# Moving the FFN row products of a decode kernel into a loop pass that skips its V products, with a new load order and a buffer of its own for w_down

## Chip, cores and metric

One core of a Trainium2 chip. The batches of experiments ran on different chips, so the ratios are to the kernel before in the same rounds. The metric is the device time of one execution in microseconds, median of several runs. "Span" is the time from the first to the last instruction of an execution; it is about 1.8 us less than the execution's time.

## The reference

A decode step for one token: grouped-query attention over a cache of 32768 positions, a SwiGLU FFN, and a sigmoid gate that mixes the two.

```python
g = sigmoid((x * gate_w).sum(-1))                    # x: 512 numbers
q = x @ wq                                           # 32 heads of 128, 8 K/V heads
a = softmax(q k^T / sqrt(128)) v @ wo                # k, v: 8 x 32768 x 128 each, bf16
b = (silu(x @ w_gate) * (x @ w_up)) @ w_down         # F = 1792
out = g * a + (1 - g) * b
```

K and V are 134 of the 148 MB that the kernel must read. Each number is used by four heads and then never again.

## The kernel before

Everything is loaded through one queue, in the order of the list `stream`. K and V come in halves of 4 MB, written K(g,half) and V(g,half) for K/V head g. Five buffers of 4 MB (the ring) take them in turn; an entry of the stream may be issued only when the entry that had its buffer before has been used up (`before` and `released`).

```python
    stream = [("wq",), ("F1",), ("K", 0, 0), ("K", 0, 1), ("F2",)]
    for g in range(1, G):
        for hf in range(2):
            stream += [("K", g, hf), ("V", g - 1, hf)]
    stream += [("V", G - 1, 0), ("V", G - 1, 1), ("wo",)]

    place = {("wq",): 1, ("F1",): 3, ("F2",): 4, ("wo",): 2}
    for g in range(G):
        for hf in range(2):
            place["K", g, hf] = 2 * hf
            place["V", g, hf] = 2 * hf + 1
    place["V", G - 1, 1] = 0
    before = {}
    for i, e in enumerate(stream):
        for d in stream[:i]:
            if place[d] == place[e]:
                before[e] = d
```

```python
            def _(sp):
                for i, e in enumerate(stream):
                    ld = sem_ld[place[e]]
                    if e in before:
                        sp.wait_ge(*released[before[e]])
    # ... cut ...
                    else:
                        kind, g, hf = e
                        src = (A_k_cache if kind == "K" else A_v_cache)[
                            0, g, hf * (S // 2) : (hf + 1) * (S // 2), :
                        ].rearrange("(p r) d -> p r d", r=RH)
                        dst = kv_slot(e)
    # ... cut ...
```

PE (TensorE) first forms q, then the FFN rows (`emit_ffn`, 32 matmuls), then runs a loop over the heads. In each pass it transposes a K half, forms the scores, and then does the V products of the previous head. In the first pass there is no previous head, so the V products are skipped.

```python
                def emit_ffn():
                    take(load_sem(("F1",)), 32)
                    for acc, wt in ((ps_g, wg), (ps_u, wu)):
                        for k in range(KC):
                            for c in range(4):
                                ins = pe.matmul(
                                    acc[32 * c : 32 * c + 1, :],
                                    xT[:, k : k + 1],
                                    wt[:, k, c * FW : (c + 1) * FW].rearrange(
                                        "d (i j) -> d j i", j=FC
                                    ),
                                    start=(k == 0),
                                    stop=(k == KC - 1),
                                )
                    ins.then_inc(sem_pe_h, 1)
```

```python
                emit_x()
                pe.wait_ge(sem_xT, 1)
                pe.wait_ge(sem_ident, 2)
                pe.wait_ge(sem_osel, 1)
                emit_q()
                emit_ffn()
                pe.sem_inc(sem_pv, 2)
                pe.wait_ge(sem_tT, 1)
                with pe.Fori(0, G) as g:
                    emit_k(0)
                    with pe.If(g > 0):
                        emit_pv(0)
                    emit_k(1)
                    with pe.If(g > 0):
                        emit_pv(1)
                    pe.sem_inc(sem_exp, -2)
                    pe.wait_ge(sem_ptc, 2)
                    pe.sem_inc(sem_ptc, -2)
                    pe.sem_inc(sem_qc, -1)
```

ACT takes the sigmoid of the FFN rows and DVE the two products and a transpose, all ahead of their own loops:

```python
                act.wait_ge(sem_qz, 4)
                emit_qc(0)
                act.wait_ge(sem_pe_h, 1)
                act.activation(sg[:, :], ps_g, ACT.Sigmoid).then_inc(sem_sg, 1)
```

```python
                dve.wait_ge(sem_sg, 1)
                dve.tensor_tensor(t1[:, :], sg[:, :], ps_g, ALU.mult).then_inc(sem_t1, 1)
                dve.wait_ge(sem_t1, 1)
                dve.wait_ge(sem_omg, 1)
                dve.scalar_tensor_tensor(
                    tr[:, :], t1[:, :], omg[:, 0:1], ps_u, ALU.mult, ALU.mult
                ).then_inc(sem_t1, 1)
                dve.wait_ge(sem_t1, 2)
                dve.transpose(tT[:, :], tr[:, :]).then_inc(sem_tT, 1)
```

After the loop come the last head's V products, the w_down products (`emit_outb`), and 64 matmuls against wo.

## Time and profile before

| | |
|---|---|
| time, median of 3 runs | 355.69 us (355.57 to 355.91) |
| the execution that was traced | 358.45 us, span 356.6 us |
| share of the span: PE, DVE, load queue | 72%, 56%, 97.1% |

Two lines of the profile page of before: busy time of PE (microseconds, share of the span), and the load queue (packets, MB, share of what 16 DMA engines could have done in the span).

```profile
PE 257.4 (72%) x2467; PEld 182.1 (51%) x2467; DVE 200.4 (56%) x373; ACT 18.5 (5%) x54; POOL 5.6 (2%) x22
...
q1 hardware_dynamic: 6050, 148.12, 97.1%
```

The chain of waits that ended last, as shares of the span by line:

```profile
by line: DMA ring<-in_A_wo_dram 7.3%; PE ps L442 2.2%; PE ps L456 0.6%; SPq L331 0.5%; DVE ktT L733 0.3%; issue 0.2%; DVE row L817 0.1%; PE ps L576 0.1%; PE ps L488 0.1%
```

The queue is nearly always busy, and the last thing that the kernel waited for was a load. So the time is that of the load stream, plus whatever stops the stream. The windows of 1 us show where it stops. Columns: start and end, length, busy time of PE, PE's weight loads, DVE, ACT and POOL with instruction counts, PE clock, DMA share, GB/s.

```profile
43.00:44.00 1.00, 1.00 (x13) 0.42 (x12) 1.00 (x2) 0.00 (x0) 0.00 (x0) 1.00 1.02 430
44.00:45.00 1.00, 1.00 (x12) 0.99 (x10) 1.00 (x3) 0.00 (x0) 0.00 (x0) 1.00 0.45 186
...
46.00:47.00 1.00, 1.00 (x14) 0.70 (x7) 0.88 (x3) 0.00 (x0) 0.00 (x0) 1.00 0.00 0
...
50.00:51.00 1.00, 0.94 (x8) 0.61 (x6) 1.00 (x3) 0.00 (x0) 0.00 (x0) 1.00 0.37 131
```

The last column goes from 430 to 0, and stays at 0 from 46 to 49 us. The timeline says why (start, length, engine, line, operation, count, idle time before it):

```profile
22.89 6.64 PE L411 MATMUL ps<-ring,xT 128*1 128x448 bf16 x32 [0.43 <-PEq L360]
...
31.52 0.65 DVE L722 STREAM_TRANSPOSE tT<-tr 128x448 bf16<-128x448 bf16 x1
...
32.60 4.50 PE L442 MATMUL ps<-ident_f,ring 128*128 128x128 f32 x20 [3.07 <-PEq L360]
...
48.77 0.33 SPq L349 DMA_DIRECT2D ring<-in_A_k_cache_dram  x1
```

The FFN rows occupy PE from 22.89 us for 6.64 us, the transpose of their product on DVE ends at 32.2 us, and only then does K(0,0) start on PE (line 442). K(1,0), which needs the buffer of K(0,0), is issued at 48.77 us. All that could be issued ahead of it, 18.1 MB, had landed by about 46 us.

The end of the kernel: the second half of the last V (line 507) is multiplied when it lands at 343.84 us, then the last o product (line 522), the 64 wo matmuls (line 576), and the output's issue.

```profile
343.84 1.04 PE L507 MATMUL ps<-ring,ET 128*16 128x512 bf16 x16 [2.23 <-DMA ring<-in_A_v_cache_dram]
...
346.02 1.84 PE L522 MATMUL ps<-osel,pv_sb 128*128 128x4 f32 x8 [1.14 <-PEq L360]
...
349.31 5.30 PE L576 MATMUL ps<-ring,O 128*1 128x256 bf16 x64 [0.67 <-DMA ring<-in_A_wo_dram]
...
355.10 0.31 SPq L351 DMA_DIRECT2D out_dram<-row  x1
```

From that landing to the output's issue it is 355.10 - 343.84 = 11.3 us. I call it the tail.

One more line is used throughout, the stretch from 44 to 74 us, in which the hole and its refilling lie:

```profile
44.00:74.00 30.00, 26.85 (x239) 19.96 (x238) 25.97 (x48) 3.20 (x7) 0.39 (x1) 0.94 0.85 356
```

### The profile page before, as it was taken

Reading aid. Unit: us, or ns where it says so; the run is one execution under the profiler, and the core shown is the slowest. Engines: PE = TensorE matmul, PEld = TensorE weight load, DVE = VectorE, ACT = ScalarE, POOL = GpSimd, SP = SyncE. Lnnn points to the kernel's source line nnn. Section 1 sums busy time; section 2 is a strip of 40 time slices with the busy share of each in tenths; the row PEclk is TensorE's granted clock in tenths of the full one; section 3 lists DMA queues with packets and bytes.
Section 4 is the critical chain, followed back from the end, with each engine's and each line's share of the span. In section 5 each row is a group of like instructions: output and inputs, shape, how many; then the busy total and the mean of one; then the engine's idle time right before and its main releaser. Section 6 shows DMA issues by size and latency. Waiting matters only on the chain. (4 is left out here: it accounts for less than half of the span.)

```text
span 356.6 us, 5752 instructions
## 1 busy us (share of the span) xinstructions
PE 257.4 (72%) x2467; PEld 182.1 (51%) x2467; DVE 200.4 (56%) x373; ACT 18.5 (5%) x54; POOL 5.6 (2%) x22
## 2 busy tenths in 40 slices
PE   0086987968669783959296775869594948887756
PEld 0043755836466453736183746656372727654343
DVE  2224688856647582839275574838382845766211
ACT  1000000300100001000100001000100010001000
POOL 0200000000000000000000000000000000000000
PEclk9997699898958996999989896978899895999687
DMA  8999959999999999999999999999999999999994
GB/s 338 404 425 459 387 196 411 452 426 419 456 419 423 452 419 441 437 415 445 434 415 448 434 412 448 434 412 448 434 412 448 434 412 452 430 415 452 408 421 197
DMA packets 6060, 148.21 MB, mean 416 GB/s; under 512 B 675, under 2 KB 678, under 8 KB 1062
## 3 DMA queue, kind: packets, MB, share of 16 engines
q1 hardware_dynamic: 6050, 148.12, 97.1%
q8 instruction: 5, 0.08, 0.1%
q14 instruction: 1, 0.01, 0.0%
q10 hardware_dynamic: 4, 0.00, 0.0%
HBM read 148.11 MB, written 0.00 MB: 415 GB/s over the span
## 5 line engine op out<-in xcount | busy, mean ns | idle before, releaser
L733 DVE COPY ktT<-ps 128x1024 bf16<-128x1024 bf16 x256 | 162.8, 684 | 89.5 <-PE ps L442 86.4
L442 PE MATMUL ps<-ident_f,ring 128*128 128x128 f32 x1024 | 159.6, 312 | 54.9 <-PEq L360 54.9
L442 PEld LDWEIGHTS ps<-ident_f,ring 128*128 128x128 f32 x1024 | 134.4, 162 | 91.8 <-issue 66.3
L456 PE MATMUL ps<-ktT,qc 128*32 128x512 bf16 x512 | 42.5, 409 | 15.2 <-DVE ktT L733 15.1
L507 PE MATMUL ps<-ring,ET 128*16 128x512 bf16 x512 | 32.3, 394 | 4.0 <-DMA ring<-in_A_v_cache_dram 2.2
L507 PEld LDWEIGHTS ps<-ring,ET 128*16 128x16 bf16 x512 | 12.6, 91 | 20.0 <-issue 7.4
L456 PEld LDWEIGHTS ps<-ktT,qc 128*32 128x32 bf16 x512 | 8.0, 95 | 28.4 <-DVE ktT L733 24.1
L738 DVE TENSOR_REDUCE pmaxf<-ps 128x1 f32<-128x512 f32 x16 | 11.1, 692 | 13.8 <-DVEq L737 13.8
L522 PEld LDWEIGHTS ps<-osel,pv_sb 128*128 128x128 f32 x80 | 14.2, 266 | 2.2 <-issue 2.2
L522 PE MATMUL ps<-osel,pv_sb 128*128 128x4 f32 x80 | 13.7, 294 | 1.6 <-PEq L360 1.6
L596 ACT ACTIVATE qc<-qz 128x112 bf16<-128x112 bf16 x8 | 2.4, 296 | 212.3 <-DVE nbias L756 199.5
L618 ACT ACTIVATE P<-ps,nbias 128x512 bf16<-128x512 f32 x16 | 10.7, 675 | 27.4 <-DVE nbias L756 27.4
L769 DVE COPY pv_sb<-ps 128x512 f32<-128x512 f32 x10 | 6.8, 682 | 6.0 <-PE ps L507 6.0
L386 PE MATMUL ps<-xT,ring 128*128 128x1 bf16 x128 | 3.6, 165 | 7.4 <-PEq L360 7.4
L488 PE MATMUL ps<-ident,P 128*128 128x128 bf16 x72 | 7.0, 220 | 1.9 <-ACT P L618 1.4
L763 DVE COPY ET<-ps 128x512 bf16<-128x512 bf16 x18 | 7.5, 415 | 1.3 <-PE ps L488 1.3
L302 POOL PARTITION_ALL_REDUCE gmax<-pmax x8 | 3.0, 373 | 309.9 <-DVE pmax L745 309.9
L386 PEld LDWEIGHTS ps<-xT,ring 128*128 128x128 bf16 x128 | 3.5, 104 | 7.4 <-issue 7.4
L411 PE MATMUL ps<-ring,xT 128*1 128x448 bf16 x32 | 6.6, 984 | 0.4 <-PEq L360 0.4
L488 PEld LDWEIGHTS ps<-ident,P 128*128 128x128 bf16 x72 | 5.4, 98 | 2.8 <-ACT P L618 1.9
L369 PE MATMUL ps<-ones_bf,x_row 1*128 1x1 bf16 x4 | 0.3, 174 | 8.7 <-DMA gw_row<-in_gate_w_dram 8.7
L576 PE MATMUL ps<-ring,O 128*1 128x256 bf16 x64 | 5.2, 334 | 0.7 <-DMA ring<-in_A_wo_dram 0.7
(75 smaller groups left out, 39.0 us busy)
## 6 DMA issues: line engine op xcount, KB each, us to landing
ring<-in_A_k_cache_dram SPq DMA_DIRECT2D x16, 4096.0 KB, 25.2
ring<-in_A_v_cache_dram SPq DMA_DIRECT2D x15, 4096.0 KB, 32.9
ring<-in_A_wq_dram SPq DMA_DIRECT2D x1, 4096.0 KB, 13.4
ring<-in_A_v_cache_dram SPq DMA_DIRECT2D x2, 2048.0 KB, 27.2
ring<-in_A_wo_dram SPq DMA_DIRECT2D x1, 2048.0 KB, 22.8
ring<-in_B_w_gate_dram SPq DMA_DIRECT2D x1, 1792.0 KB, 17.3
ring<-in_B_w_up_dram SPq DMA_DIRECT2D x1, 1792.0 KB, 21.1
ring<-in_B_w_down_dram SPq DMA_DIRECT2D x1, 1792.0 KB, 43.4
```

Of the source, the lines that this page charges most:

```text
L386: ins = pe.matmul(ps_m[:, M_Q0 + h : M_Q0 + h + 1], wq_v[:, c, h * DH : (h + 1) * DH], xT[:, c : c + 1], start=(c == 0), stop=(c == KC - 1),)
L411: ins = pe.matmul(acc[32 * c : 32 * c + 1, :], xT[:, k : k + 1], wt[:, k, c * FW : (c + 1) * FW].rearrange("d (i j) -> d j i", j=FC), star ...
L442: ins = pe.transpose(stb[:, t * 64 : (t + 2) * 64], two.bitcast(FP32), ident_f[:, :])
L456: ins = pe.matmul(ps_sc[hf][32 * c : 32 * c + 32, :], qc[:, e, 24 - PB * i : 56 - PB * i], kt[:, e, :], start=(i == 0 and e == 0), stop=(i ...
L488: ins = pe.transpose(ps_pt[:, hf * 512 + m * 128 : hf * 512 + (m + 1) * 128], P[:, hf, m * 128 : (m + 1) * 128], ident[:, :],)
L507: ins = pe.matmul(ps_pv[32 * c : 32 * c + 2 * PB, :], ET[:, hf, col : col + 2 * PB], src[:, i0 : i0 + 2, c, 2 * m : 2 * m + 2, :].rearrang ...
L522: ins = pe.matmul(ps_m[:, M_OT : M_OT + HPG], pv_sb[:, r * DH : (r + 1) * DH], osel[:, r * HPG : (r + 1) * HPG], start=(r == 0), stop=(r = ...
L618: act.activation(P[:, hf, :], ps_sc[hf], ACT.Exp, bias=nbias[:, 0:1], scale=SCALE, accum_out=esum[:, g, hf : hf + 1],).then_inc(sem_exp, 1)
L733: dve.tensor_copy(ktT[:, q % NKT, :], pst[q % NST]).then_inc(sem_cp, 1)
L738: ins = dve.tensor_reduce(pmaxf[:, hf : hf + 1], ps_sc[hf], AX.X, ALU.max)
L763: dve.tensor_copy(ET[:, hf, :], ps_pt[:, hf * 512 : (hf + 1) * 512]).then_inc(sem_ptc, 1)
L769: dve.tensor_copy(pv_sb[:, :], ps_pv).then_inc(sem_pvc, 1)
```

## The change

Three parts. The FFN rows move on PE from ahead of the loop into its first pass, in place of the skipped V products of half 0, between K(0,0) and K(0,1); their sigmoid and products on ACT and DVE move likewise. w_gate and w_up are loaded behind K(0,0) instead of ahead of it. w_down gets a buffer of its own, so that w_gate/w_up can have the fifth slot of the ring. (PSUM banks move to fit, and three scratch tiles move into the buffer of V(0,1), whose load therefore waits for `sem_tT`.)

```diff
-    stream = [("wq",), ("F1",), ("K", 0, 0), ("K", 0, 1), ("F2",)]
+    stream = [("wq",), ("K", 0, 0), ("F1",), ("K", 0, 1), ("F2",)]
...
-    place = {("wq",): 1, ("F1",): 3, ("F2",): 4, ("wo",): 2}
+    place = {("wq",): 1, ("F1",): 4, ("wo",): 2}
...
+        wd_t = T("wd_t", [128, FC, NOUT], BF16)
...
                     if e in before:
                         sp.wait_ge(*released[before[e]])
+                    elif e == ("V", 0, 1):
+                        sp.wait_ge(sem_tT, 1)
...
                 emit_q()
-                emit_ffn()
                 pe.sem_inc(sem_pv, 2)
-                pe.wait_ge(sem_tT, 1)
                 with pe.Fori(0, G) as g:
                     emit_k(0)
                     with pe.If(g > 0):
                         emit_pv(0)
+                    with pe.Else():
+                        emit_ffn()
+                        pe.wait_ge(sem_t1, 2)
                     emit_k(1)
... (DVE: the same products as emit_t(), called in the first pass)
                         emit_k(hf, each)
+                        if hf == 0:
+                            with dve.If(it == 0):
+                                emit_t()
```

Bytes loaded, matmuls and elementwise work are the same. The intent is that K(0,0) reaches PE sooner, so that its buffer is free before the stream runs dry.

More of the change, by code (lines that the diff above doesn't have):

```diff
@@ L82, in bass_gated_mix__gqa_block_cached__swiglu_ffn__decode_kernel @@
         for d in stream[:i]:
-            if place[d] == place[e]:
+            if e in place and place.get(d) == place[e]:
                 before[e] = d
@@ L95, in bass_gated_mix__gqa_block_cached__swiglu_ffn__decode_kernel @@
         sem_ldv = S_("s_ldv")
+        sem_f2 = S_("s_f2")
         sem_ldo = [S_(f"s_ldo{i}") for i in range(len(WO_CUT))]
@@ L179, in bass_gated_mix__gqa_block_cached__swiglu_ffn__decode_kernel @@
         qc = T("qc", [128, 2, 56], BF16)
-        sg = T("sg", [128, FW], FP32)
-        t1 = T("t1", [128, FW], FP32)
-        tr = T("tr", [128, FW], BF16)
         tT = T("tT", [128, FW], BF16)
@@ L218, in bass_gated_mix__gqa_block_cached__swiglu_ffn__decode_kernel @@
         assert M_O0 + WOJ <= 512
-        ps_g = ps[:, NST, 0:FW]
-        ps_u = ps[:, NST + 1, 0:FW]
+        ps_g = ps[:, 4, 0:FW]
+        ps_u = ps[:, 5, 0:FW]
         ps_a = ps[:, 1, 0:OW]
@@ L224, in slot_of @@
             return ring[:, place[entry], :]
+        sg = ring[:, 3, 0 : 2 * FW].bitcast(FP32)
+        t1 = ring[:, 3, 1024 : 1024 + 2 * FW].bitcast(FP32)
+        tr = ring[:, 3, 2048 : 2048 + FW]
         def kv_slot(entry):
@@ L232, in bass_gated_mix__gqa_block_cached__swiglu_ffn__decode_kernel @@
         wu = f1[:, KC * F : 2 * KC * F].rearrange("p (c f) -> p c f", c=KC)
-        wd = slot_of(("F2",))[:, 0 : FC * NOUT].rearrange("p (j n) -> p j n", j=FC)
+        wd = wd_t[:, :, :]
         wo_v = slot_of(("wo",))[:, 0 : WOJ * NOUT].rearrange("p (j n) -> p j n", j=WOJ)
@@ L308, in _ @@
                 for i, e in enumerate(stream):
-                    ld = sem_ld[place[e]]
+                    ld = sem_ld[place[e]] if e in place else sem_f2
                     if e in before:
                         sp.wait_ge(*released[before[e]])
+                    elif e == ("V", 0, 1):
+                        sp.wait_ge(sem_tT, 1)
                     if e[0] == "wq":
@@ L422, in emit_outb @@
                 def emit_outb():
-                    pe.wait_ge(load_sem(("F2",)), 16)
+                    pe.wait_ge(sem_f2, 16)
+                    pe.wait_ge(sem_tT, 1)
                     for j in range(FC):
@@ L599, in _ @@
                 emit_qc(0)
-                act.wait_ge(sem_pe_h, 1)
-                act.activation(sg[:, :], ps_g, ACT.Sigmoid).then_inc(sem_sg, 1)
                 def emit_oc(n):
@@ L610, in _ @@
                 emit_oc(1)
+                act.wait_ge(sem_pe_h, 1)
+                act.activation(sg[:, :], ps_g, ACT.Sigmoid).then_inc(sem_sg, 1)
                 for g in range(G):
@@ L639, in _ @@
                 dve.memset(ps[:, 6:8, :], 0.0).then_inc(sem_pv0, 1)
-                dve.memset(ps[:, NST : NST + 2, :], 0.0).then_inc(sem_pv0, 1)
+                dve.memset(ps[:, 4:6, :], 0.0).then_inc(sem_pv0, 1)
                 dve.memset(P[:, :, :], 0.0).then_inc(sem_exp, 2)
@@ L712, in _, with emit_t @@
                 ).then_inc(sem_omg, 1)
-                dve.wait_ge(sem_sg, 1)
-                dve.tensor_tensor(t1[:, :], sg[:, :], ps_g, ALU.mult).then_inc(sem_t1, 1)
-                dve.wait_ge(sem_t1, 1)
-                dve.wait_ge(sem_omg, 1)
-                dve.scalar_tensor_tensor(
-                    tr[:, :], t1[:, :], omg[:, 0:1], ps_u, ALU.mult, ALU.mult
-                ).then_inc(sem_t1, 1)
-                dve.wait_ge(sem_t1, 2)
-                dve.transpose(tT[:, :], tr[:, :]).then_inc(sem_tT, 1)
+                def emit_t():
+                    dve.wait_ge(sem_sg, 1)
+                    dve.tensor_tensor(t1[:, :], sg[:, :], ps_g, ALU.mult).then_inc(sem_t1, 1)
+                    dve.wait_ge(sem_t1, 1)
+                    dve.scalar_tensor_tensor(
+                        tr[:, :], t1[:, :], omg[:, 0:1], ps_u, ALU.mult, ALU.mult
+                    ).then_inc(sem_t1, 1)
+                    dve.wait_ge(sem_t1, 2)
+                    dve.transpose(tT[:, :], tr[:, :]).then_inc(sem_tT, 1)
+                dve.wait_ge(sem_omg, 1)
                 def local(k, ins):
```

## The prediction

> **What bounds the kernel.** The load stream. The profile's queue table shows the DMA queue at 97.1% of 16 engines' span, moving 148.12 MB; the chain that ended last is the landing of the last weight wo (26.02 us of waiting on DMA, then 0.4 us matmul, 0.4 us copy). Busy shares are lower: PE 72%, DVE 56%. [...]from 60 us to 350 us the windows of this trace average about 425 GB/s[...].
>
> **Where it stops.** Once. Windows of 1 us show 430 GB/s until 44 us, then 186, 86, 0, 0, 0, 393, 131 until 51 us. That is 0.80 MB where 425 GB/s would carry 2.98 MB: 5.1 us lost. Cause: the five loads issued in the first 4 us (wq, w_gate/w_up, K(0,0), K(0,1), w_down: 18.1 MB) have drained, and the next load, K(1,0), needs K(0,0)'s slot. The list of DMA issues shows it issued only at 48.77 us, when K(0,0)'s last scores run. The timeline shows why: K(0,0) starts on PE at 32.6 us and takes 16.2 us (clock 0.5 for 9.8 us of it). It starts late for two reasons of about equal size: it queues behind w_gate/w_up (landed at 22.7 us; 4.19 MB more at 425 GB/s is 32.6 us), and PE does q, the FFN rows (6.64 us, 22.9 to 29.5) and waits for sigmoid/products/transpose until 32.2 us.
>
> **What the change does.** Same bytes, same matmuls. K(0,0) is now second in the queue: wq plus K(0,0) are 8.39 MB, landing at about 24 us; q is ready at 23.7 us. K(0,0) then runs from about 24.3 us for 13 to 16 us, so K(1,0) is issued at 38 to 41 us, 4 to 6 us before the queue drains at 44 to 45 us. The 5.1 us hole closes, and all of it is on the critical path, since everything after is one continuous stream.
>
> The FFN moves between K(0,0) and K(0,1): 6.64 us, then about 2.2 us wait for sigmoid 0.54, product 0.62, second product 0.68 and semaphores. K(0,1) starts at 47 to 50 us (before: 48.9) and ends at 60 to 64 us. Its slot is needed for K(1,1) when K(1,0)+V(0,0) (8.39 MB, 19.7 us) have drained: about 64.4 us. This is the thin spot: 0 to 4 us of slack. If the clock is low there ([...]0.50 follows the 3 us idle at 29.5 us), 1 to 3 us of a new hole can open. V(0,1) waits for the FFN transpose at about 50 us: no cost. The DVE/PE branches of later passes are off the path: PE needs about 14 us per K half, the stream 19.7 us.
>
> **Predicted.** 355.7 - 5.1 + 0.2 (chance of a small new hole) = 350.8 us, a gain of 1.4%. Range 349.8 to 352.8. Even a perfect stream cannot reach -2% (348.6 us): 148.12 MB at 425 GB/s is 348.5 us before start and tail. Faster by over 2%: 0.03; within 2%: 0.95; slower: 0.02.
>
> **Signs.** Right: K(1,0) issued at about 39 us; no window of zero GB/s from 44 to 51 us; DMA share nearer 98.5%; FFN row matmuls at about 39 to 46 us; K(1,1) issued by 64 us; the last chain still wo. Wrong: K(1,0) issued after 44 us; a hole near 64 to 67 us; a lower rate after 50 us.
>
> **What would make it wrong.** PE cold throughout the first pass, making K(0,0) plus FFN plus K(0,1) exceed the 40 us between 24 and 64 us; a rate that depends on order or buffer; the end becoming bound by PE rather than by wo.

That the stream can't be sped up was not shown. What the traces show is that before and after the change it moved 432 GB/s from 74 to 300 us.

## The result, and the profile after

| | before | changed |
|---|---|---|
| median of 6 runs | 355.78 us (355.55 to 357.13) | 353.16 us (352.58 to 354.19) |
| ratio, 95% interval | | 0.9924 (0.9902 to 0.9945) |
| execution traced | 358.45 us | 353.63 us |

A ratio here is the mean time of one kernel's fast runs over that of the other's in the same rounds, so it isn't quite the ratio of the medians. The change gains 2.6 us, 0.8%. The forecast was 4.9 us (350.8 us, range 349.8 to 352.8): the direction and the class were right, the size was not, and 353.16 lies outside the range.

The same lines of the page and of the chain of waits:

```profile
PE 255.6 (73%) x2467; PEld 179.2 (51%) x2467; DVE 200.5 (57%) x373; ACT 18.5 (5%) x54; POOL 5.6 (2%) x22
...
q1 hardware_dynamic: 6050, 148.12, 98.2%
```

```profile
by line: PE ps L584 1.6%; PE ps L529 0.5%; DVE row L829 0.1%; issue 0.1%; DVE O2a L825 0.1%; PE ps L575 0.1%; DVE O L827 0.1%; DVE oTs L821 0.0%; DVEq L820 0.0%
```

The queue's share rose from 97.1 to 98.2%. The chain no longer ends in a load but on PE, in the wo matmuls (line 584) and the last o product (line 529). That was not forecast.

The windows in which the stream had stopped:

```profile
43.00:44.00 1.00, 1.00 (x8) 0.00 (x0) 0.00 (x0) 0.00 (x0) 0.00 (x0) 1.00 0.97 416
44.00:45.00 1.00, 0.57 (x4) 0.00 (x0) 0.00 (x0) 0.38 (x1) 0.00 (x0) 1.00 1.20 514
...
47.00:48.00 1.00, 1.00 (x10) 1.00 (x11) 0.62 (x2) 0.00 (x0) 0.00 (x0) 1.00 0.91 393
...
50.00:51.00 1.00, 1.00 (x6) 0.87 (x5) 0.84 (x2) 0.00 (x0) 0.00 (x0) 0.50 1.14 492
```

The hole is gone: the lowest of these eight windows, 47 to 48 us, has 393 GB/s. The timeline shows the forecast order of events:

```profile
24.30 3.93 PE L449 MATMUL ps<-ident_f,ring 128*128 128x128 f32 x20 [2.54 <-PEq L366]
...
37.80 0.33 SPq L355 DMA_DIRECT2D ring<-in_A_k_cache_dram  x1
...
37.94 6.64 PE L417 MATMUL ps<-ring,xT 128*1 128x448 bf16 x32
...
46.57 0.65 DVE L729 STREAM_TRANSPOSE tT<-ring 128x448 bf16<-128x448 bf16 x1
...
46.92 4.35 PE L449 MATMUL ps<-ident_f,ring 128*128 128x128 f32 x24 [2.35 <-PEq L366]
...
59.64 0.33 SPq L355 DMA_DIRECT2D ring<-in_A_k_cache_dram  x1
```

K(0,0) starts at 24.30 us (forecast 24.3), K(1,0) is issued at 37.80 (38 to 41), the FFN rows run from 37.94 to 44.6 (39 to 46), K(0,1) starts at 46.92 (47 to 50), K(1,1) is issued at 59.64 (by 64). So the mechanism is as told, and in the two traced executions even the size is right: 358.45 - 353.63 = 4.8 us. But the medians differ by 2.6 us only. Where are the other 2.2? (That the traced pair agrees so well is partly luck: by the measure of the next section its hole was 5.6 us and its end grew by 0.9, and 5.6 - 0.9 = 4.7.)

The end of the changed kernel, as shown for before:

```profile
338.18 1.89 PE L514 MATMUL ps<-ring,ET 128*16 128x512 bf16 x16 [2.22 <-DMA ring<-in_A_v_cache_dram]
...
341.21 1.84 PE L529 MATMUL ps<-osel,pv_sb 128*128 128x4 f32 x8 [1.14 <-PEq L366]
...
344.11 5.72 PE L584 MATMUL ps<-ring,O 128*1 128x256 bf16 x64 [0.28 <-DVE O L827]
...
350.31 0.32 SPq L357 DMA_DIRECT2D out_dram<-row  x1
```

The tail is 350.31 - 338.18 = 12.1 us here, 0.9 us longer than in the trace of before. The last V half's products took 1.89 us instead of 1.04, the wo matmuls 5.72 instead of 5.30.

The stretch from 44 to 74 us of the changed kernel:

```profile
44.00:74.00 30.00, 24.47 (x184) 18.45 (x180) 21.85 (x38) 3.75 (x8) 0.39 (x1) 0.83 1.02 437
```

### The profile page after: what moved, and what is told of

Read it like the earlier page. It is cut to its first block, busy times and chain, and to the rows that moved or that the text cites. A ratio compares the mean times of both kernels' runs of the same rounds, so it can differ in the third digit from the quotient of the medians.

```text
span 351.8 us, 5768 instructions
## 1 busy us (share of the span) xinstructions
PE 255.6 (73%) x2467; PEld 179.2 (51%) x2467; DVE 200.5 (57%) x373; ACT 18.5 (5%) x54; POOL 5.6 (2%) x22
## 3 DMA queue, kind: packets, MB, share of 16 engines
q1 hardware_dynamic: 6050, 148.12, 98.2%
## 5 line engine op out<-in xcount | busy, mean ns | idle before, releaser
L449 PE MATMUL ps<-ident_f,ring 128*128 128x128 f32 x1024 | 157.9, 309 | 52.2 <-PEq L366 51.0
L449 PEld LDWEIGHTS ps<-ident_f,ring 128*128 128x128 f32 x1024 | 131.9, 160 | 89.1 <-issue 63.6
L514 PEld LDWEIGHTS ps<-ring,ET 128*16 128x16 bf16 x512 | 12.8, 92 | 21.4 <-issue 8.9
L747 DVE TENSOR_REDUCE pmaxf<-ps 128x1 f32<-128x512 f32 x16 | 11.1, 692 | 13.7 <-DVEq L746 13.7
L529 PEld LDWEIGHTS ps<-osel,pv_sb 128*128 128x128 f32 x80 | 13.3, 250 | 3.0 <-issue 3.0
L529 PE MATMUL ps<-osel,pv_sb 128*128 128x4 f32 x80 | 12.9, 284 | 1.8 <-PEq L366 1.8
L625 ACT ACTIVATE P<-ps,nbias 128x512 bf16<-128x512 f32 x16 | 10.8, 676 | 28.2 <-DVE nbias L765 28.2
```

The source lines that it names most:

```text
L449: ins = pe.transpose(stb[:, t * 64 : (t + 2) * 64], two.bitcast(FP32), ident_f[:, :])
L514: ins = pe.matmul(ps_pv[32 * c : 32 * c + 2 * PB, :], ET[:, hf, col : col + 2 * PB], src[:, i0 : i0 + 2, c, 2 * m : 2 * m + 2, :].rearrang ...
L529: ins = pe.matmul(ps_m[:, M_OT : M_OT + HPG], pv_sb[:, r * DH : (r + 1) * DH], osel[:, r * HPG : (r + 1) * HPG], start=(r == 0), stop=(r = ...
L625: act.activation(P[:, hf, :], ps_sc[hf], ACT.Exp, bias=nbias[:, 0:1], scale=SCALE, accum_out=esum[:, g, hf : hf + 1],).then_inc(sem_exp, 1)
L747: ins = dve.tensor_reduce(pmaxf[:, hf : hf + 1], ps_sc[hf], AX.X, ALU.max)
```

## The experiments

Two theories to begin with. A: the hole of 5.1 us belongs to a long execution (358.45 us), while the median runs have a smaller one, because the PE clock during K(0,0) differs between executions. B: the hole is always 5.1 us and the changed kernel gives 2.3 us back, at its end. A third, C, came from my own forecast: in some executions a new hole opens ahead of K(1,1).

In the traces of the kernel before, the clock column shows 0.50 in the low stretches and 1.00 elsewhere, with values between in the 1 us windows that only part of a stretch falls into. The low stretches at K(0,0), summed from those windows, are 3.40 us long in b_t1, 6.82 in b_same and 10.24 in before and b_t2, that is about one, two or three times 3.4 us. Below I call 3.4 us of it a low window. What sets their number was not shown: in the trace of before PE is busy throughout from 34.82 to 38.23 us, and the clock stays at 0.50 until 41.64. (The prediction read the longest one as 9.8 us. It begins at 31.40 us, within the idle time of PE from 29.53 to 32.60 us, so that 9.0 us of it fall into K(0,0).)

To compare traces I use one measure of lost stream time. In the changed kernel the stretch from 44 to 74 us carries 437 GB/s, so a kernel with x GB/s there lost 30 us x (437 - x) / 437. It includes the uneven first microseconds after a stop, so it is a little more than the prediction's count from 44 to 51 us: 5.6 us for the first trace of before where that gave 5.1.

### b_same, b_t1, b_t2: the kernel before, traced three more times

No edit.

> The kernel before, unchanged, for a second trace. Theory A (the first trace was of a long execution: 358.45 us where the timed runs had 355.7): times 355.5 to 357, this trace's execution is nearer to 355.7, its span nearer 353.9 than 356.6, K(1,0) is issued 2 to 3 us earlier than 48.77 us, because K(0,0) met less of the 0.5 clock than 9.8 us, and the hole in the stream is about 2 to 3 us, not 5.1. Theory B (the hole is 5.1 us in every run and the changed kernel gives 2.3 us back at its end): K(1,0) is issued at 48.5 to 49 us whatever the run's time.

> The kernel before, unchanged, a third trace. Theory A: whatever its time, the clock is 0.5 for a whole number of 3.3 us steps in K(0,0) (three in the trace I predicted from, two in the second), K(1,0) is issued 1.4 to 2 us earlier per step less, and the execution's time less its loss (bytes moved by 120 us, against the changed kernel's 50.9 MB, at 432 GB/s) is 352 to 353.5 us.

> The kernel before, unchanged, a fourth trace; the same expectation. If the times of these two differ by 1 us or more, the issue time of K(1,0) differs in the same direction by about as much.

Measured: b_same 356.33 us median of 6 (355.81 to 357.13), ratio 1.0003 (0.9977 to 1.0028) to the kernel before. Its trace is of a run of 356.67 us, with two low windows and K(1,0) issued at 47.32 us. b_t1 took 355.76 us, one low window, issued at 46.32. b_t2 took 358.23 us, three low windows, issued at 48.98. Two lines of b_t1's timeline and its stretch from 44 to 74 us:

```profile
32.72 4.03 PE L442 MATMUL ps<-ident_f,ring 128*128 128x128 f32 x20 [3.73 <-PEq L360]
...
46.32 0.33 SPq L349 DMA_DIRECT2D ring<-in_A_k_cache_dram  x1
```

```profile
44.00:74.00 30.00, 25.88 (x236) 18.69 (x239) 25.03 (x45) 3.20 (x7) 0.39 (x1) 0.94 0.94 392
```

The first 20 transposes of K(0,0) take 4.03 us here; they take 4.50 in the trace of before, and the issue comes 2.45 us earlier. The stretch carries 392 GB/s, not 356, so the loss is 3.1 us, not 5.6. An execution of the median's length has little more than half of the hole that I had measured. Theory A holds. One expectation was too large: K(1,0) came 1.45 us earlier with the first window less, but only 1.0 us with the second, not 1.4 to 2 us each time.

### b_warm: no idle PE ahead of K(0,0)

```diff
+                def warm(n):
+                    for _ in range(n):
+                        pe.transpose(ps[:, 2, 0:128], ident_f[:, :], ident_f[:, :])
                 emit_ffn()
+                warm(17)
                 pe.sem_inc(sem_pv, 2)
```

> The kernel before with 17 idle-filling transposes on PE (2.5 us, results unused) between the FFN rows and the wait for the transposed product, so that PE doesn't idle for 3 us before K(0,0). Same loads, same order. Theory A (hole size is set by the clock in K(0,0)): clock 1.0 in 32 to 45 us, K(0,0) takes about 13 us, K(1,0) is issued at about 45.5 us, hole about 1.5 us, time 1 to 2 us under the kernel before, i.e. about 354. If the clock doesn't matter: time as before, 355.7, K(1,0) at 48 to 49 us.

```profile
29.22 2.08 PE L533 MATMUL ps<-ident_f 128*128 128x128 f32 x17
...
32.70 2.67 PE L442 MATMUL ps<-ident_f,ring 128*128 128x128 f32 x20 [1.40 <-PEq L360]
...
45.36 0.33 SPq L349 DMA_DIRECT2D ring<-in_A_k_cache_dram  x1
```

```profile
44.00:74.00 30.00, 25.65 (x248) 18.41 (x248) 24.63 (x44) 3.20 (x7) 0.39 (x1) 0.94 0.97 408
```

Measured: 355.08 us median (354.76 to 355.95), ratio 0.9971 (0.9945 to 0.9996). No low window falls in K(0,0) (the clock column is at 1.00 from 32 to 46 us), its first 20 transposes take 2.67 us instead of 4.03 to 4.50, K(1,0) is issued at 45.36 us, and the loss is 2.0 us. Nothing was moved in the kernel, only PE was kept from idling (1.40 us idle just before K(0,0) instead of 3.07), and 1.1 us of the median went away (356.19 us before in the same rounds; the interval just excludes 1). The spread shrank too: its six runs lie within 1.2 us, the eleven of the kernel before within 2.9. So the clock sets a good part of the hole. The "about 354" missed, since the kernel before was slower in these rounds than in the first. Even at full clock a hole remains, since K(0,0) reaches PE at 32.7 us.

### b_ffn2: more hole

```diff
-                def emit_ffn():
+                def emit_ffn(times=1):
                     take(load_sem(("F1",)), 32)
-                    for acc, wt in ((ps_g, wg), (ps_u, wu)):
+                    for acc, wt in ((ps_g, wg), (ps_u, wu)) * times:
...
-                emit_ffn()
+                emit_ffn(2)
```

> The kernel before with its FFN rows computed twice (6.64 us more on PE ahead of K(0,0)). Theory A: K(0,0) starts at 38.9 us instead of 32.6, K(1,0) issued at 52 to 55 us, hole 7.5 to 11 us, time 360.5 to 364; time minus hole 352.5 to 353.5 as in every other kernel, so a microsecond of hole is a microsecond of time. If part of a hole is regained later in the stream: clearly less than 5 us over the kernel before.

Measured: 362.21 us median (361.01 to 365.68), ratio 1.0193 (1.0146 to 1.0240). K(1,0) at 51.70 us, 309 GB/s from 44 to 74 us, a loss of 8.8 us in a run of 361.01 us. The issue is 0.3 us earlier than expected, time and loss are in their ranges. Time less loss is 352.2 us, close to the 352.4 to 352.7 of the kernel before (see the table): a microsecond of hole costs a microsecond of time, and nothing is regained later.

### a_ffnearly and a_oldorder: one part of the change alone

a_ffnearly keeps the new load order and puts the FFN back ahead of the loop on all engines. a_oldorder keeps the FFN in the loop and restores the load order:

```diff
# a_ffnearly
                 emit_q()
+                emit_ffn()
                 pe.sem_inc(sem_pv, 2)
+                pe.wait_ge(sem_tT, 1)
...
-                    with pe.Else():
-                        emit_ffn()
-                        pe.wait_ge(sem_t1, 2)
... (sigmoid and products ahead of the loops of ACT and DVE again)
# a_oldorder
-    stream = [("wq",), ("K", 0, 0), ("F1",), ("K", 0, 1), ("F2",)]
+    stream = [("wq",), ("F1",), ("K", 0, 0), ("K", 0, 1), ("F2",)]
```

> Only the new load order: the changed kernel with FFN rows, sigmoid and products ahead of the loop as before. Theory A: the FFN rows must now wait for w_gate/w_up, which land at about 32.3 us behind K(0,0); rows until 39, product transposed at 41.6, K(0,0) from 41.6 to 54.5 or later, K(1,0) issued at 54.5 to 57.5 us, hole 10 to 13 us, time 363 to 366: slower than the kernel before by 2 to 3%. Time minus hole stays 352.5 to 353.5.

> Only the FFN move: the changed kernel with the old load order (wq, w_gate/w_up, K(0,0), K(0,1), w_down). Theory A (one hole, sized by when K(0,0) is done on PE): K(0,0) lands at 32.6 us as before and starts then, after 10 us of PE idling, so that the clock is likely 0.5 at its start; K(1,0) issued at 45.5 to 49 us, hole 2 to 5 us, time 355 to 357, no gain over the kernel before. If the FFN rows alone were the cause: a gain of 2 us or more.

Measured, a_ffnearly: 365.53 us median of 5 (365.06 to 367.17), ratio 1.0268 (1.0233 to 1.0303), as expected. K(1,0) issued at 55.89 us; the stretch from 44 to 74 us:

```profile
44.00:74.00 30.00, 26.65 (x229) 20.52 (x228) 25.81 (x47) 3.20 (x7) 0.39 (x1) 0.92 0.61 251
```

At 251 GB/s the loss is 12.8 us.

Measured, a_oldorder: 358.91 us median (357.40 to 360.89), ratio 1.0072 (1.0031 to 1.0112). My expectation of "no gain" missed: it is slower than before by 2.2 us. The timeline:

```profile
32.73 4.50 PE L449 MATMUL ps<-ident_f,ring 128*128 128x128 f32 x20 [10.95 <-PEq L366]
...
46.92 0.33 SPq L355 DMA_DIRECT2D ring<-in_A_k_cache_dram  x1
...
47.05 6.62 PE L417 MATMUL ps<-ring,xT 128*1 128x448 bf16 x32
...
56.02 3.26 PE L449 MATMUL ps<-ident_f,ring 128*128 128x128 f32 x24 [2.34 <-PEq L366]
...
67.67 0.33 SPq L355 DMA_DIRECT2D ring<-in_A_k_cache_dram  x1
```

K(0,0) starts no earlier than before (32.73 us; its first 20 transposes take 4.50 us, as in the trace of before, where the clock was at 0.50), because it is still behind w_gate/w_up in the queue, and K(1,0) is issued at 46.92 us. But now the FFN rows stand between K(0,0) and K(0,1), so that K(0,1) starts at 56.02 us and K(1,1) is issued at 67.67 us, late enough to dent the stream a second time (164 GB/s from 67 to 68 us). I had overlooked that; together the loss is 5.5 us.

So neither part gains by itself: each is a loss without the other. K(0,0) has to be early in the queue and early on PE.

### a_ffn2: how much slack the changed kernel has

The same edit as b_ffn2, in the changed kernel.

> The changed kernel with its FFN rows computed twice (same result, 6.64 us more on PE between K(0,0) and K(0,1)). It tests the slack that my prediction called thin, which the trace of the changed kernel shows as about 4 us (K(1,1) issued at 59.6 us, stream empty at about 63.7). Expected: K(1,1) issued at 66 to 67.5 us, a hole of 2 to 4 us at 64 to 68 us, time 355 to 357, i.e. 2 to 3.5 us over the changed kernel. If PE in the first pass has more slack than I think, or none: 0, or 6.6 us.

Measured: 356.20 us median (355.77 to 359.13), 1.0016 (0.9978 to 1.0054) of before, as expected. K(1,1) at 65.71 us (expected 66 to 67.5), 396 GB/s, a loss of 2.8 us. Of 6.64 us more on PE about 3.8 us went into slack.

### a_same, a_t1, a_t2, a_t3: the changed kernel, traced four more times

No edit.

> The changed kernel, unchanged, for a second trace and the spread of its runs. Theory A: about 353.2 us, no hole at 44 to 51 us nor at 64 us. Theory B: the same time, and the chain that ended last is PE's wo matmuls at clock 0.5, ending 1.5 to 2.5 us after the last landing plus the 0.85 us of the last matmuls and copy. Theory C (in other executions a new hole opens before K(1,1)): this trace, or the slow ones of its runs, show K(1,1) issued after 64 us and a window under 200 GB/s there.

> The changed kernel, unchanged, a third trace and six more times. Its runs so far fall into two groups, about 352.6 and 354.4 us. If theory B holds in this reduced form (the clock in the last stage decides between the two): a trace with a time near 352.6 shows the second V half's products at clock 1.0 (1.04 us, not 1.89), the last o product at 1.03 us, not 1.84, and 10.8 to 11.3 us from the landing of V's last half to the issue of the output, not 12.1; a trace near 354.4 shows 12.1.

> The changed kernel, unchanged, a fourth trace and six more times in the same rounds as a_tail3. Reduced theory B: time 352.4 to 354.5, as before. If its trace is of a run under 353 us, the second V half's products take 1.04 us and V landing to output issue is 10.8 to 11.3 us; if over 353.5 us, 1.89 us or a cold stretch in the wo matmuls, and 12 us or more.

> The changed kernel, unchanged, a fifth trace: the same expectation. In both, no window from 44 to 51 us under 250 GB/s, and K(1,0) issued by 41 us whether K(0,0) ran at the low clock (its transposes then take 4.5 us for the first 20, as in the third trace) or at the high one (under 4).

Measured: medians 353.63 us (a_same, 352.43 to 354.47; 0.9920 of before, interval 0.9889 to 0.9950), 353.21 (a_t1, 352.45 to 355.39; 0.9881, 0.9830 to 0.9933) and 353.31 (a_t2, 352.57 to 354.54; 0.9917, 0.9887 to 0.9947); a_t3 once, 353.54. None has a hole at 44 to 51 us. In a_t1 and a_t2 K(0,0) ran as slowly as at 0.50 in the trace of before (4.50 us for the first 20 transposes, 2.67 at 1.00 in b_warm). That is the ground on which I take its clock to be low: the clock column shows 1.00 from 8 to 44 us in both. K(1,0) was issued at 40.55 and 40.04 us, and it cost no hole there: the change takes the speed of K(0,0) off the critical path in these two. But in a_t1 the delay went on to K(1,1):

```profile
24.41 4.50 PE L449 MATMUL ps<-ident_f,ring 128*128 128x128 f32 x20 [3.33 <-PEq L366]
...
40.55 0.33 SPq L355 DMA_DIRECT2D ring<-in_A_k_cache_dram  x1
...
62.43 0.33 SPq L355 DMA_DIRECT2D ring<-in_A_k_cache_dram  x1
```

K(1,1) at 62.43 us was late enough to dent the stream (197 GB/s from 63 to 64 us, 420 from 44 to 74, a loss of 1.2 us) in a run of 355.39 us; at 61.89 us in a_t2 it was not. That is theory C in a mild form, in one of five traces: the expectation had asked for an issue after 64 us.

The gain itself depends on the rounds: in those of a_t1 the medians were 357.10 and 353.21 us, a gain of 3.9 us, because the kernel before had more long runs there (up to 360.38 us).

The trace of a_t2 is of a run of 352.57 us, and its end looks like this:

```profile
338.46 1.04 PE L514 MATMUL ps<-ring,ET 128*16 128x512 bf16 x16 [0.66 <-DMA ring<-in_A_v_cache_dram]
...
340.65 1.02 PE L529 MATMUL ps<-osel,pv_sb 128*128 128x4 f32 x8 [1.15 <-PEq L366]
...
343.45 5.32 PE L584 MATMUL ps<-ring,O 128*1 128x256 bf16 x64 [1.02 <-DMA ring<-in_A_wo_dram]
...
349.26 0.32 SPq L357 DMA_DIRECT2D out_dram<-row  x1
```

Here the tail is 349.26 - 338.46 = 10.8 us: 1.04 us for V, 1.02 for o, 5.32 for wo. In the run of 353.63 us shown above it was 12.1. In a_t3 (11.9 us) V and o were as short as here, but wo took 6.45 us; in a_t1 (12.5 us) V took 1.04, o 1.84 and wo 6.47 us. The clock records that were read fit the reduced theory B only in part. In the two traces with 12.1 us, of changed and a_same, the clock is at 0.50 for 10.24 us, about from V's landing on, that is for three windows. But before and b_warm have 6.82 us at 0.50 in their last stage too, and tails of 11.3 and 10.8 us. For a_t1, a_t2 and a_t3 the clock of the last stage was not read. So an end that is up to 1.7 us later goes with longer products, and in two of the four late traces with the low clock. This is read from traces; the interventions of the next section did not confirm it in the times.

The chain that ended last is on PE in a_same as well; in a_t1, a_t2 and a_t3 the wait for wo leads it (6.2, 6.4 and 5.7% of the span), as the prediction had it. The chains of b_warm and b_ffn2 end on PE too, with a tail of 10.8 us: where the chain ends doesn't tell by itself how long the tail is.

### a_tailwarm, a_tail2, a_tail3: a shorter tail

```diff
# a_tailwarm (warm as in b_warm)
                             emit_outb()
+                            warm(14)
                             pe.wait_ge(sem_ldv, 16)
...
                 emit_pv(1, halves=True)
+                warm(6)
                 emit_o()
+                warm(3)
                 pe.wait_ge(sem_oT2, 1)
# a_tail2: as a_tailwarm, with warm(20), and emit_outb() moved up:
+                emit_outb()
                 emit_pt(0)
...
-                            emit_outb()
+                            warm(20)
# a_tail3: as a_tail2, and
-    WO_CUT = (16, 8, 4, 2, 2)
+    WO_CUT = (6, 8, 8, 6, 4)
```

> The changed kernel with idle-filling transposes on PE in the last stage (14 ahead of the wait for the last half of V, 6 ahead of the last o product, 3 behind it), so that the clock stays at 1.0 for the 64 wo matmuls. Theory B (the end on PE at clock 0.5 eats part of the gain): the wo matmuls wait for the last landing again, the chain ends in DMA, time 1 to 1.5 us under the changed kernel, about 352. Theory A alone: at most 0.5 us under the changed kernel.

> The changed kernel with the w_down products moved from the last stage's busiest point to the start of it, where PE waits for the exponentials (1.7 us less ahead of the last V half), and idle-filling transposes (20, 6, 3) so that the clock is 1.0 when the last V half lands. Unlike the earlier try, PE should be ahead of the stream, so that the filling delays nothing. Reduced theory B: the upper group of times goes away, about 352.5 us, 0.7 to 1 us under the changed kernel; from landing of V's last half to issue of the output 10.8 us. If the tail isn't it: 353.5 as the changed kernel.

> a_tail2 with the five wo loads cut 6, 8, 8, 6, 4 instead of 16, 8, 4, 2, 2: in a_tail2's trace the 64 wo matmuls waited 1.0 us for the first 16 and then ran 5.3 us without a break, ending 1 us after the last landing. Expected: wo matmuls start about 0.8 us earlier and end with the last landing, 0.5 to 0.8 us under a_tail2, about 352.1 us, and no run over 353. If the landing of V or wo bounds the end wholly: as a_tail2, 352.7.

Measured: a_tailwarm 353.44 us (352.44 to 354.61; 0.9919, 0.9890 to 0.9948) against a_same's 353.63 in the same rounds: short of the 1 to 1.5 us expected, and inconclusive. In its trace PE was late, the filling began only at 338.54 us, and V's products waited for its end until 340.22. Nor did the filling hold the clock at 1.00: it is at 0.50 for 3.40 us from 344.7 us on, under the wo matmuls, which took 5.33 us all the same. a_tail2 352.72 us (352.52 to 353.70; 0.9873, 0.9822 to 0.9924) against a_t1's 353.21, 0.5 us where 0.7 to 1 was expected. a_tail3 353.01 us (352.61 to 354.35; 0.9913, 0.9883 to 0.9942) against a_t2's 353.31. a_tail3's trace does what was meant:

```profile
338.27 1.04 PE L514 MATMUL ps<-ring,ET 128*16 128x512 bf16 x16 [1.43 <-DMA ring<-in_A_v_cache_dram]
...
342.53 1.69 PE L591 MATMUL ps<-ring,O 128*1 128x256 bf16 x28 [0.28 <-DVE O L834]
...
348.21 0.60 PE L591 MATMUL ps<-ring,O 128*1 128x256 bf16 x8 [0.41 <-DMA ring<-in_A_wo_dram]
...
349.30 0.32 SPq L357 DMA_DIRECT2D out_dram<-row  x1
```

The wo matmuls start within 4.3 us of V's landing, wait for the later pieces of wo (0.90, 0.84 and 0.41 us), and end with the last. Yet the tail is 11.0 us, no better than a good run of the changed kernel: with V and o as short as in a_t2 (1.04 and 1.03 us), the landing of wo bounds the end. My expectation of 352.1 us and no run over 353 missed; two of its six runs took 353.8 and 354.4, and what lengthened those was not traced. The best versions lie 0.3 to 0.5 us under the changed kernel in their rounds, which their intervals don't tell apart from it.

### All traces in one table

Columns: low-clock windows in K(0,0), counted for the kernel before and b_warm only; when K(1,0) was issued; GB/s from 44 to 74 us; the loss worked out from it; the tail; the time of that execution; and that time less the loss and less the tail's excess over 10.8 us.

| trace | low windows | K(1,0) at, us | GB/s | loss, us | tail, us | time, us | rest, us |
|---|---|---|---|---|---|---|---|
| before | 3 | 48.77 | 356 | 5.6 | 11.3 | 358.45 | 352.4 |
| b_t2 | 3 | 48.98 | 356 | 5.6 | 10.9 | 358.23 | 352.6 |
| b_same | 2 | 47.32 | 376 | 4.2 | 10.8 | 356.67 | 352.5 |
| b_t1 | 1 | 46.32 | 392 | 3.1 | 10.8 | 355.76 | 352.7 |
| b_warm | 0 | 45.36 | 408 | 2.0 | 10.8 | 355.05 | 353.1 |
| b_ffn2 | - | 51.70 | 309 | 8.8 | 10.8 | 361.01 | 352.2 |
| a_ffnearly | - | 55.89 | 251 | 12.8 | 10.8 | 365.22 | 352.4 |
| a_oldorder | - | 46.92 | 357 | 5.5 | 11.5 | 359.72 | 353.5 |
| a_ffn2 | - | 38.30 | 396 | 2.8 | 12.0 | 355.81 | 351.8 |
| changed | - | 37.80 | 437 | 0 | 12.1 | 353.63 | 352.3 |
| a_same | - | 38.19 | 441 | -0.3 | 12.1 | 354.47 | 353.4 |
| a_t1 | - | 40.55 | 420 | 1.2 | 12.5 | 355.39 | 352.5 |
| a_t2 | - | 40.04 | 437 | 0 | 10.8 | 352.57 | 352.6 |
| a_t3 | - | 38.00 | 437 | 0 | 11.9 | 353.54 | 352.4 |
| a_tail3 | - | 37.93 | 439 | -0.1 | 11.0 | 352.61 | 352.5 |

Times from 352.6 to 365.2 us become rests from 351.8 to 353.5, most of them within 0.4 us of 352.5. Two terms, the loss early and the tail late, explain nearly all of the differences. (In a_tailwarm and a_tail2 the filling hides when V landed, so they have no tail. In a_oldorder too PE came to V's products without a wait, so that V may have landed earlier and its 11.5 is a lower bound. In a_ffn2 the 12.0 comes from a load: its last four wo matmuls waited for the last piece of wo until 351.53 us, 11.1 us after V's landing.) a_same's rest, 0.9 us above 352.5, is not explained.

## Why the prediction was wrong

Right, as shown by the traces: the kernel is bound by its load stream (the queue at 97.1 and 98.2% of the span); the stream stops once, because K(1,0) waits for K(0,0); both the queue order and the FFN on PE delay K(0,0) (each part undone gave the hole back or enlarged it); the change closes the hole; every forecast instant was met to about 1.4 us (the FFN rows ended at 44.6 us, not 46); the thin spot at K(1,1) is real (a_ffn2, a_t1).

The step that failed is the sum "355.7 - 5.1 + 0.2 (chance of a small new hole) = 350.8 us". Its middle term was mis-sized. The 5.1 us were measured in an execution of 358.45 us and taken off the median of other executions, which was 355.69. In an execution of that length (b_t1, 355.76 us) the same count, 44 to 51 us, gives 264 GB/s, hence 7 us x (425 - 264) / 425 = 2.65 us. Had the 5.1 us been taken off the execution in which they were measured, the sum would have been 358.45 - 5.1 + 0.2 = 353.55 us, and the trace of the changed kernel took 353.63. The last term was about right: the five traces of the changed kernel lost 0, -0.3, 1.2, 0 and 0 us from 44 to 74 us, 0.2 on average.

Why the hole differs was shown: one, two or three low-clock windows in K(0,0) give losses of 3.1, 4.2 and 5.6 us, none gives 2.0, and the intervention that removed them shortened the kernel. The prediction saw the low clock ("clock 0.5 for 9.8 us of it") and did not ask whether the next execution would have it.

A smaller term was absent: the tail. With the hole as counted by the prediction the sum would have been 355.69 - 2.65 + 0.2 = 353.2 us, which is the measured 353.16. By the wider measure (3.1 us) it would have been 352.8, and 0.4 us is left, for which the tail is the candidate: in four of the five traces it is 11.9 to 12.5 us, 1.1 to 1.7 above the shortest, while the six traces of before with and without its edits had 10.8 to 11.3. The prediction's sign "the last chain still wo" failed in this trace and in a_same, where three low windows (10.24 us at 0.50) set in as V landed, and held in the other three. Whether the new timing makes a longer tail more likely, or whether five and six traces just fell so, stays open; so do two runs of before at 360.3 us in the batch of a_t1, which were not traced.

One figure of the prediction is a little low: the trace of before averages 431 GB/s from 60 to 350 us, not about 425. The hole changes by less than 0.1 us with it, but the floor of 348.5 us does not stand, since 148.12 MB at 431 GB/s take 343.7 us. That the gain stays under 2% is better read from the table: without loss and at the shortest tail most traces leave 352.4 to 352.7 us.

## What to carry to other kernels

Subtract a loss that was read in a trace from the time of the execution that was traced, never from the median of others; and if the two times differ by half of the expected gain, find out which one is usual before forecasting, by tracing again. When a stream of loads is the limit, look for the one moment at which it runs dry and trace back what held the buffer; moving work and moving its load had to go together here, as each alone made this kernel slower (1.0268 and 1.0072 of before). An engine at 72% busy still set the time through the moment at which it freed a buffer (K(1,0) at 48.77 us), and with it its clock did (a loss of 5.6 us with 10.24 us at 0.50, of 2.0 us with none).
